# Shifted copies of score tiles moved from VectorE to GpSimd as 32-bit integer adds, in an order that treats the shared SBUF port as a lock

## The chip, the cores and the metric

The kernel runs on one core of one Trainium2 chip. Times are device microseconds. A median is over the runs of one kernel. A ratio is the mean time of one kernel's fast runs over that of the kernel before in the same rounds, with a 95% interval, so it is not quite the ratio of the medians that are quoted. The span of a profile is 1 to 3 us shorter than the time of its run.

A core has TensorE (PE), ScalarE (ACT), VectorE (DVE), GpSimd (POOL) and the DMA queues. They run side by side and wait for each other through semaphores; a port to the on-chip memory SBUF that VectorE and GpSimd share makes those two wait as well, and this case is about it. PSUM is the other on-chip memory; this kernel uses it in banks, and TensorE writes all its results there.

## The reference, cut to what matters

Two independent parts are computed and laid side by side in the output. The first is a state-space layer (2048 steps, 640 channels). The second is an attention layer with 32 heads that share one key and one value head:

```python
q = (x @ wq).reshape(B, S, 32, 20).transpose(0, 2, 1, 3)
k = x @ wk ; v = x @ wv
scores = einsum("bhqd,bkd->bhqk", q, k) * 20 ** -0.5
p = softmax(scores)
o = einsum("bhqk,bkd->bhqd", p, v) ; out = o.transpose(...).reshape(...) @ wo
```

With 32 heads, 16 blocks of 128 keys and 4 blocks of 512 queries there are 32 x 16 x 4 = 2048 score tiles of 128x512, and each element of them needs an exponential.

## The kernel before

A Python program (the planner) plays through the kernel with planned durations: at each step it gives a free engine the most urgent piece of work that is ready. It then writes out one fixed instruction order for each engine, with the semaphores that this order needs. The plan decides, tile by tile, who makes the exponentials:

* **ScalarE tiles.** TensorE writes scores into PSUM in chunks of three and two tiles. ScalarE takes the exponential of a chunk, from PSUM into SBUF. TensorE then multiplies it with the values.
* **VectorE tiles.** TensorE writes one score tile to a PSUM bank. VectorE adds a constant and stores it as a 16-bit integer, whose bits read as bf16 are a rough exponential ("eviction" below). Three more copies of the tile, with 32, 64 and 96 added, are made from SBUF to SBUF. TensorE multiplies all four with scaled values and sums them, which averages the error. Such a tile costs four value products in place of one.

```python
class Build:
    CHUNKS = (3, 2)     # PSUM banks of ScalarE's two score slots
    MISC = 2            # PSUM banks for VectorE tiles AND all background work
    NDS = 18            # SBUF buffers for evicted and copied tiles
    SHARE = 0.25        # at most this share of the tiles goes to VectorE
    SHIFTS = ((0, 0.2421875), (32, 0.201171875), (64, 0.169921875), (96, 0.142578125))
    # ... cut

    def want_d(self, taken=0):           # may the next tile be a VectorE tile?
        s = self.s
        if self.tile_n >= NTILE - 8 or self.d_count + taken + 1 > self.SHARE * (self.tile_n - 16):
            return False
        if len(self.d_banks()) <= taken:                           # a free PSUM bank
            return False
        return len(self.d_free()) > taken + len(self.SHIFTS) - 1    # free SBUF buffers

    def fill_d(self, op, m):
        # ... cut
        first = self.dve(self.ts(p.DR[:, h.index, :], bank.ap, 16256.0, 0.0, ALU.add, ALU.max), 605, deps=[op],
                         reads=[bank.key], writes=[key], prio=self.P1)
        self.s.spawn(self.d_give(bank, first))
        self.d_open.append([h, first, list(range(1, n)), b, kc, j])
        self.d_left[b, j] += n - 1
        self.pv_entry(b, kc, j, 0, h, first)

    def copy(self, op, k, tiles):        # one copy, or two tiles in one instruction
        # ... cut
        op.fns.append(self.ts(at(dst), at(src), float(self.SHIFTS[k][0]), 0.0, ALU.add, ALU.max))
```

The two `MISC` banks also serve the background work: query projections, the state-space products and the output projections. The number of VectorE tiles, D below, is thus fixed when the program is written out.

## Time and profile before

Median 787.37 us (786.44 to 789.14, 4 runs). In the profile (span 786.0 us):

| quantity | value | where it is read |
|---|---|---|
| ScalarE busy | 764.3 us, 97% | page, part 1 |
| ScalarE's exponentials | 1652 tiles, 747.4 us, 0.452 us each | groups |
| VectorE busy | 736.9 us, 94% | page, part 1 |
| VectorE tiles | 396 of 2048 (19.3%) | groups, evictions |
| GpSimd busy | 13.5 us, 2% | page, part 1 |

The page's busy line of the kernel before, then three of its groups. In a group, the columns are line, engine, operation, output and input, shapes and count; then busy time, mean ns of one; then idle time of the engine just before, and who ended it.

```profile
PE 727.8 (93%) x10253; PEld 237.8 (30%) x10253; DVE 736.9 (94%) x1765; ACT 764.3 (97%) x686; POOL 13.5 (2%) x35
...
L1015 ACT ACTIVATE PR<-SC 128x1024 bf16<-128x1024 f32 (+1 forms) x661 | 747.4, 1456 | 4.9 <-PE MB L546 2.6
...
L561 DVE TENSOR_SCALAR DR<-MB 128x512 int16<-128x512 f32 x396 | 262.7, 680 | 16.2 <-PE MB L546 14.1
L561 DVE TENSOR_SCALAR DR<-DR 128x512 int16<-128x512 int16 (+1 forms) x821 | 239.2, 342 | 2.9 <-PE MB L546 0.4
```

661 exponentials make 1652 tiles. The chain that ended last, by engine, and then the same engines in three steady stretches (busy us of each stretch; the count of instructions in brackets; PEclk is the granted share of TensorE's full clock):

```profile
ACT 90%; PE 5%; DVE 3%; DMA 1%; issue 0%; ACTq 0%; DVEq 0%
```

```profile
core 0: us, PE busy (x) PEld busy (x) DVE busy (x) ACT busy (x) POOL busy (x), PEclk, DMA share, GB/s
170.00:400.00 230.00, 217.41 (x3127) 70.29 (x3123) 221.86 (x507) 229.47 (x204) 0.00 (x0) 1.00 0.07 18
400.00:550.00 150.00, 142.86 (x2087) 46.34 (x2091) 143.84 (x343) 150.00 (x135) 0.00 (x0) 1.00 0.09 21
550.00:740.00 190.00, 176.83 (x2569) 57.26 (x2561) 178.02 (x426) 189.53 (x169) 0.00 (x0) 1.00 0.06 18
```

ScalarE is full in the steady stretches: 229.47 of 230, 150.00 of 150, 189.53 of 190. It is what bounds the kernel. So the span can be written as 786.0 - 747.4 = 38.6 us of start and tail, plus 0.4524 us for each of the 2048 - D tiles that are not among the D VectorE tiles. What this change can do is to raise D, unless it makes ScalarE wait.

VectorE's timeline from 100 us shows what a VectorE tile costs when instructions follow each other:

```profile
start us, us, engine line op out<-in xcount [idle before <-releaser]
...
100.02 1.27 DVE L561 TENSOR_SCALAR DR<-MB 128x512 int16<-128x512 f32 x2
101.22 0.41 DVE L561 TENSOR_SCALAR DR<-DR 128x1024 int16<-128x1024 int16 x1
...
103.76 1.08 DVE L561 TENSOR_SCALAR DR<-DR 128x1024 int16<-128x1024 int16 x3
104.76 0.68 DVE L561 TENSOR_SCALAR DR<-MB 128x512 int16<-128x512 f32 x1
```

Two evictions reach from 100.02 to 101.22, so 0.60 us each; three pair copies reach from 103.76 to 104.76, where the next instruction starts, so about 0.335 each.

The start of the trace has an instance that fits the shared port. The first line is GpSimd's timeline, the second VectorE's:

```profile
12.25 1.67 POOL L561 TENSOR_SCALAR fr<-iota,sc 128x512 int32<-128x512 f32 x2 [3.35 <-DVE sc L560]
```

```profile
12.66 0.71 DVE L560 TENSOR_SCALAR aq<-QT 128x512 int16<-128x512 int16 x1
```

The mask (`aq`) of 128x512 on VectorE takes 0.71 us while GpSimd works, where its group mean is 0.296 us.

### The profile page before, as it was taken

What the parts mean: (1) busy time and instruction counts of PE and PEld (TensorE: products, weight loads), DVE (VectorE), ACT (ScalarE), POOL (GpSimd) and SP (SyncE); (2) the same over time, 40 slices, a digit from 0 to 9 for tenths busy, and PEclk for the clock granted to TensorE, in tenths of its full rate; (3) what the DMA queues carried; (4) which work ended last, traced back from release to release, by engine and by line L of the source; (5) the groups of instructions that cost most, each with busy time, mean ns of one, the idle gap of its engine ahead of it and who ended that gap; (6) DMA issues with size and microseconds to landing.
All of it is one profiled execution on the core that took longest, in us unless ns stands there. A gap on an engine that the chain in (4) does not pass through costs nothing.

```text
span 786.0 us, 23805 instructions
## 1 busy us (share of the span) xinstructions
PE 727.8 (93%) x10253; PEld 237.8 (30%) x10253; DVE 736.9 (94%) x1765; ACT 764.3 (97%) x686; POOL 13.5 (2%) x35
## 2 busy tenths in 40 slices
PE   8988998889988999999999999999998999899887
PEld 3322222222223332323323222223222322233223
DVE  5999999999999999999998999999899999988995
ACT  5899999999999999999999999999999999999995
POOL 6000000000000000000000000000000000000000
PEclk9999999999999999999999999999999999999999
DMA  9840000020000000010000000010000000000001
GB/s 209 122 87 8 9 9 8 9 45 9 9 9 16 23 9 29 17 42 23 10 15 16 23 23 22 19 33 17 10 16 8 23 23 15 22 24 22 16 6 39
DMA packets 54184, 21.57 MB, mean 27 GB/s; under 512 B 43464, under 2 KB 54080, under 8 KB 54080
## 3 DMA queue, kind: packets, MB, share of 16 engines
q1 hardware_dynamic: 52072, 19.87, 11.4%
q8 instruction: 81, 1.33, 0.7%
q10 hardware_dynamic: 2008, 0.18, 0.2%
q14 instruction: 23, 0.19, 0.1%
HBM read 7.20 MB, written 5.50 MB: 16 GB/s over the span
## 4 chain that ended last, share of the span: by engine, by line
ACT 90%; PE 5%; DVE 3%; DMA 1%; issue 0%; ACTq 0%; DVEq 0%
ACT PR L1015 89%; PE SC L546 2%; PE MB L546 2%; DVE DR L561 1%; PE MB L542 1%; DMA vrow<-in_A_Dskip_dram 1%; PE SC L542 1%; DVE prod L556 0%; DVE WO L691 0%; DVE xbT L768 0%; DMA dn<-sums 0%; DMA sums<-pvsb 0%; ACTq L527 0%; DVE fr L561 0%; DVE g L1503 0%
## 5 line engine op out<-in xcount | busy, mean ns | idle before, releaser
L1015 ACT ACTIVATE PR<-SC 128x1024 bf16<-128x1024 f32 (+1 forms) x661 | 747.4, 1456 | 4.9 <-PE MB L546 2.6
L546 PE MATMUL SC<-QT,KT 32*128 32x512 bf16 x1652 | 257.8, 384 | 46.8 <-ACT PR L1015 33.0
L561 DVE TENSOR_SCALAR DR<-MB 128x512 int16<-128x512 f32 x396 | 262.7, 680 | 16.2 <-PE MB L546 14.1
L561 DVE TENSOR_SCALAR DR<-DR 128x512 int16<-128x512 int16 (+1 forms) x821 | 239.2, 342 | 2.9 <-PE MB L546 0.4
L546 PE MATMUL MB<-DR,VS 128*32 128x512 bf16 x1584 | 230.8, 384 | 0.2 <-DVE DR L561 0.2
L546 PE MATMUL MB<-PR,VP 128*32 128x512 bf16 x1652 | 226.6, 386 | 2.4 <-DVE pvsb L1207 1.8
L546 PEld LDWEIGHTS SC<-QT,KT 32*128 32x128 bf16 x1652 | 66.5, 91 | 298.6 <-ACT PR L1015 227.5
L546 PE MATMUL MB<-QT,KT 32*128 32x512 bf16 x396 | 143.8, 384 | 2.0 <-DVE DR L561 1.0
L546 PEld LDWEIGHTS MB<-PR,VP 128*32 128x32 bf16 x1652 | 56.8, 94 | 69.7 <-issue 50.3
L546 PEld LDWEIGHTS MB<-DR,VS 128*32 128x32 bf16 x1584 | 56.6, 94 | 55.6 <-issue 33.8
L542 PE MATMUL MB<-xaT,BT 128*32 128x512 bf16 x800 | 60.5, 382 | 0.2 <-DVE DR L561 0.2
L556 DVE TENSOR_TENSOR prod<-MB,Z 128x1024 bf16<-128x1024 f32 x40 | 48.6, 1216 | 2.7 <-PE MB L542 2.2
L546 PE MATMUL MB<-xbT,wqf 128*32 128x512 bf16 x640 | 47.9, 389 | 0.3 <-DVE DR L561 0.2
L542 PE MATMUL MB<-WO,OT 128*32 128x128 bf16 (+1 forms) x928 | 41.8, 292 | 0.0
L546 PEld LDWEIGHTS MB<-QT,KT 32*128 32x128 bf16 x396 | 34.2, 91 | 19.9 <-DVE DR L561 9.0
L1503 DVE TENSOR_TENSOR_SCAN g<-sc,hst,u 128x512 bf16<-128x512 f32 x30 | 38.0, 1273 | 0.0
L546 PE MATMUL MB<-KT,VZ 128*32 128x256 bf16 x656 | 33.8, 274 | 0.0
L542 PE MATMUL MB<-CT,xbT 128*32 128x512 bf16 (+1 forms) x640 | 31.9, 301 | 0.0
L542 PE MATMUL MB<-CT,W 128*32 128x512 bf16 (+1 forms) x640 | 31.5, 301 | 0.0
L556 DVE TENSOR_TENSOR prod<-g,tab 128x1024 bf16<-128x1024 bf16 x40 | 27.0, 680 | 0.0
L1207 DVE CAST pvsb<-MB 128x512 bf16<-128x512 f32 x32 | 21.9, 683 | 5.2 <-PE MB L546 5.2
L1326 DVE CAST stg<-MB 128x512 bf16<-128x512 f32 x35 | 23.9, 682 | 1.0 <-PE MB L542 0.8
(122 smaller groups left out, 340.9 us busy)
## 6 DMA issues: line engine op xcount, KB each, us to landing
out_dram<-stg SPq DMA_DIRECT2D x35, 128.0 KB, 1.7
rdB<-recs SPq DMA_DIRECT2D x124, 32.0 KB, 1.9
CT<-in_B_x_dram SPq DMA_DIRECT2D x2, 640.0 KB, 5.7
WO<-in_B_wo_dram SPq DMA_DIRECT2D x4, 200.0 KB
wqf<-in_B_wq_dram SPq DMA_DIRECT2D x1, 680.0 KB, 5.5
out_dram<-PR SPq DMA_DIRECT2D x5, 128.0 KB, 2.4
sums<-pvsb SPq DMA_DIRECT2D x31, 4.0 KB
dn<-sums SPq DMA_DIRECT2D x31, 4.0 KB, 1.8
```

What stands on the lines that cost most here:

```text
L542: r = e.matmul(out[32 * j:32 * j + 32], lhsT=lhsT[:, 32 * j:32 * j + 32], rhs=rhs, start=start, stop=stop, tile_position=(0, 32 * j), skip ...
L546: return lambda e: e.matmul(out, lhsT=lhsT, rhs=rhs, start=start, stop=stop, **kw)
L556: return lambda e: e.tensor_tensor(out, a, b, op)
L561: return lambda e: e.tensor_scalar(out, a, s1, s2, op0=op0, op1=op1)
L1015: ex = self.act(lambda e: e.activation(dst, t[:, 0:512 * n], ACT.Exp, scale=1.0 / UNIT), 0.8333 * 512 * n + 50, deps=[op], reads=[b.key fo ...
L1207: ev = self.dve(lambda e: e.tensor_copy(p.pvsb[:, slot, :], bank.ap), 620, deps=[op], reads=[bank.key], writes=[f"pvsb{slot}"], prio=self. ...
L1326: ev = self.dve(lambda e: e.tensor_copy(st, bank.ap), 620, deps=[prev], reads=[bank.key], writes=[key], prio=self.EV, gate=(lambda: last.e ...
L1503: o = self.dve(lambda e, ri=ri, init=init: e.tensor_tensor_scan(p.g[:, u, ri, :], rdec, p.u[:, ri, :], init, ALU.mult, ALU.add), 1280, dep ...
```

## The change

GpSimd, idle so far, shall make most of the copies. Two 16-bit values are added at once as one 32-bit integer add, since the sums never carry from the low half into the high one; two tiles go into one instruction. VectorE copies only when at least nine copies are waiting, or to close a block. GpSimd and those VectorE operations that use VectorE's second SBUF port exclude each other, so the plan gives every operation a mark `port` and never runs two marked ones on the two engines at once. Core of the diff (the mark `port=True` on a dozen more lines of VectorE operations is cut):

```diff
@@ Schedule.begin
+        if op.port:
+            if eng == "pool" and self.port_last["dve"] is not None:
+                op.after.append(self.port_last["dve"])
+            self.port_free[eng] = self.t + op.dur + (self.LOCK if eng == "pool" else 0.0)
+            self.port_last[eng] = op
+            # ... cut
@@ Schedule.pick
             if r <= t + 1e-6:
+                if op.port:
+                    if self.port_free["pool" if eng == "dve" else "dve"] > t + 1e-6:
+                        if eng == "dve":
+                            held.append(op)
+                        continue
+                    if eng == "pool" and self.port_wanted:
+                        continue
                 can.append(op)
+        # ... cut: port_wanted, true while VectorE holds back more urgent port work
@@ copy_source
+        if sum(len(d[2]) for d in can) < self.BACKLOG and not (can[0][3] == self.pv_b and self.pv_filled[self.pv_b] == 64):
+            return None
-        return Op("dve", [], 200 if one else 333, prio=prio, hook=lambda op: self.copy(op, k, two))
+        return Op("dve", [], 200 if one else 333, prio=prio, port=True, hook=lambda op: self.copy(op, k, two))
+    BACKLOG = 9
+    def pool_source(self):
+        # ... cut: two tiles that need the same shift, two free buffers, else None
+        return Op("pool", [], self.POOL2, prio=1, port=True, hook=lambda op: self.copy(op, k, two, True))
+    POOL2 = 1040.0
@@ copy
+            add = bass.AP(tensor=p.step, offset=k, ap=[[4, 128], [0, 2], [0, 256]])
+            op.fns.append(self.tt(words(dst), words(src), add, ALU.add))
@@ background
-                T.append((t, 1, lambda b=8 * qb + gg: self.tile_n >= 64 * (b - 11), ...
+                T.append((t, 1, lambda b=8 * qb + gg: self.tile_n >= 64 * (b - 11) and all((b // 8, c) in self.xb_op for c in range(NC)), ...
```

The Trainium skill, "GPSIMD Engine Reference", section "Engine selection", states that a GpSimd add with both inputs and the output of one 32-bit integer type is an exact integer add.

More of the change, by code (lines that the diff above doesn't have):

```diff
@@ L24 @@
     __slots__ = ("eng", "fns", "dur", "deps", "prio", "reads", "writes", "prev", "gate", "hook", "start", "end",
-                 "seq", "land", "dma_key", "idx", "tail", "mode", "load", "late")
+                 "seq", "land", "dma_key", "idx", "tail", "mode", "load", "late", "port", "after")
     def __init__(self, eng, fns, dur, deps=(), prio=5, reads=(), writes=(), prev=None, gate=None, hook=None,
-                 dma_key=None, land=0.0, tail=0.0, mode="F", load=0.0):
+                 dma_key=None, land=0.0, tail=0.0, mode="F", load=0.0, port=False):
         self.eng, self.fns, self.dur = eng, list(fns), dur
@@ L34, in __init__ @@
         self.mode, self.load, self.late = mode, load, False
+        self.port, self.after = port, []
         self.start = self.end = None
@@ L53 @@
     PAUSE = 3300.0
+    LOCK = 60.0
     def __init__(self):
@@ L68, in __init__ @@
         self.slack = {"pe": 60.0, "dve": 150.0}
+        self.port_free = {"dve": 0.0, "pool": 0.0}
+        self.port_last = {"dve": None, "pool": None}
+        self.port_wanted = False
     def recent(self, span):
@@ L126, in begin @@
             self.loads.append((self.t, op.load))
+        if op.port:
[3 more added lines that the diff above has]
+            self.port_last[eng] = op
+            self.at(self.port_free[eng])
         if op.dma_key is not None:
@@ L147, in pick @@
                 cands = cands + [extra]
-        can = []
+        can, held = [], []
         for op in cands:
@@ L171, in pick @@
                 best, key = op, (p, op.seq)
+        if eng == "dve":
+            self.port_wanted = any(best is None or op.prio < best.prio for op in held)
         return best
@@ L246, in dep @@
                     need[src] = o
+            for o in op.after:
+                dep(o)
             for k in op.writes:
@@ L468, in alloc @@
         self.lift = sb(o, "lift", [128, 4], FP32)
+        self.step = sb(o, "step", [128, 4], I32)
         self.mab = sb(o, "mab", [128, 8], FP32)
@@ L598, in program @@
         self.s.sources["dve"].append(self.copy_source)
+        self.s.sources["pool"].append(self.pool_source)
     def warm_source(self):
@@ L661, in constants @@
         many("VS", fns, 250)
+        many("step", [lambda e, k=k, c=c: e.memset(p.step[:, k:k + 1], c * 65537) for k, (c, _) in enumerate(self.SHIFTS)], 100)
         many("VZ", [lambda e: e.memset(p.VZ[:], 0.0)], 100)
@@ L891, in qt_task @@
         aq = self.dve(self.ts(p.aq[:, gg % 4, :].bitcast(I16), dst.bitcast(I16), 0x7FFF, None, ALU.bitwise_and), 200,
-                      deps=[ev], reads=[key],
+                      deps=[ev], reads=[key], port=True,
                       writes=[f"aq{gg % 4}"], prio=0.4 if first else 2, gate=lambda: self.aq_free(qb, gg))
@@ L1132, in copy_source, with copy @@
             prio = self.CLOSE
-        return Op("dve", [], 200 if one else 333, prio=prio, hook=lambda op: self.copy(op, k, two))
-    def copy(self, op, k, tiles):
+        return Op("dve", [], 200 if one else 333, prio=prio, port=True, hook=lambda op: self.copy(op, k, two))
+    BACKLOG = 9
+    def pool_source(self):
+        s = self.s
+        can = [d for d in self.d_open if d[1].end is not None and s.seen(d[1], "pool") <= s.t]
+        if not can or len(self.d_free()) < 2:
+            return None
+        k = can[0][2][0]
+        two = [d for d in can if k in d[2]][:2]
+        if len(two) < 2:
+            return None
+        return Op("pool", [], self.POOL2, prio=1, port=True, hook=lambda op: self.copy(op, k, two, True))
+    POOL2 = 1040.0
+    def copy(self, op, k, tiles, pool=False):
         p = self
@@ L1144, in at, with words @@
             return bass.AP(tensor=p.DR, offset=512 * x[0], ap=[[512 * p.NDS, 128], [512 * (x[1] - x[0]), 2], [1, 512]])
-        op.fns.append(self.ts(at(dst), at(src), float(self.SHIFTS[k][0]), 0.0, ALU.add, ALU.max))
+        if pool:
+            def words(x):
+                return bass.AP(tensor=p.DR, offset=512 * x[0], ap=[[512 * p.NDS, 128], [512 * (x[1] - x[0]), 2], [1, 512]]).bitcast(I32)
+            add = bass.AP(tensor=p.step, offset=k, ap=[[4, 128], [0, 2], [0, 256]])
+            op.fns.append(self.tt(words(dst), words(src), add, ALU.add))
+            op.reads.append("step")
+        else:
+            op.fns.append(self.ts(at(dst), at(src), float(self.SHIFTS[k][0]), 0.0, ALU.add, ALU.max))
         op.reads += [f"DR{i}" for i in src]
@@ L1237, in normalize @@
         ot = b % 10
-        self.norm_op[b] = self.dve(self.tt(p.OT[:, ot, :], p.pvsb[:, slot, :], p.rdB[:, slot, :], ALU.mult), 350, deps=[o],
+        self.norm_op[b] = self.dve(self.tt(p.OT[:, ot, :], p.pvsb[:, slot, :], p.rdB[:, slot, :], ALU.mult), 350, deps=[o], port=True,
                                    reads=[pv, rb], writes=[f"OT{ot}"], prio=self.EV, gate=lambda: self.ot_free(b))
@@ L1437, in ssm_scalars @@
             zs = []
-            o = self.dve(self.ts(t0, sin, gim, None, ALU.mult), 250, deps=[tabs[c], sc_op] + ([o] if c else []), reads=[tk, "sc"],
+            o = self.dve(self.ts(t0, sin, gim, None, ALU.mult), 250, port=True, deps=[tabs[c], sc_op] + ([o] if c else []), reads=[tk, "sc"],
                          writes=["prod3"], prio=3)
@@ L1441, in ssm_scalars @@
             o = self.dve(lambda e, c=c, cos=cos, gre=gre, t0=t0: e.scalar_tensor_tensor(
-                out=p.Z[:, 0, c, :], in0=cos, scalar=gre, in1=t0, op0=ALU.mult, op1=ALU.add), 650, deps=[o],
+                out=p.Z[:, 0, c, :], in0=cos, scalar=gre, in1=t0, op0=ALU.mult, op1=ALU.add), 650, deps=[o], port=True,
                 reads=[tk, "sc", "prod3"], writes=[zk], prio=3)
             zs.append(o)
-            o = self.dve(self.ts(t1, sin, gre, None, ALU.mult), 250, deps=[o], reads=[tk, "sc"], writes=["prod3"],
+            o = self.dve(self.ts(t1, sin, gre, None, ALU.mult), 250, port=True, deps=[o], reads=[tk, "sc"], writes=["prod3"],
                          prio=3)
@@ L1448, in ssm_scalars @@
             o = self.dve(lambda e, c=c, cos=cos, gim=gim, t1=t1: e.scalar_tensor_tensor(
-                out=p.Z[:, 1, c, :], in0=cos, scalar=gim, in1=t1, op0=ALU.mult, op1=ALU.subtract), 650, deps=[o],
+                out=p.Z[:, 1, c, :], in0=cos, scalar=gim, in1=t1, op0=ALU.mult, op1=ALU.subtract), 650, deps=[o], port=True,
                 reads=[tk, "sc", "prod3"], writes=[zk], prio=3)
@@ L1454, in ssm_scalars @@
             self.tab_op[c] = o
-        self.neg_op = self.dve(self.ts(p.CT[:, 1, :, :], p.CT[:, 1, :, :], -1.0, None, ALU.mult), 900,
+        self.neg_op = self.dve(self.ts(p.CT[:, 1, :, :], p.CT[:, 1, :, :], -1.0, None, ALU.mult), 900, port=True,
                                deps=[self.ct_op[1]], reads=["CT1"], writes=["CT1"], prio=3)
@@ L1495, in unit_rest @@
         for ri, op in ((0, ALU.subtract), (1, ALU.add)):
-            us.append(self.dve(self.tt(p.u[:, ri, :], p.prod[:, 0, ri, :], p.prod[:, 1, ri, :], op), 350, deps=prods,
+            us.append(self.dve(self.tt(p.u[:, ri, :], p.prod[:, 0, ri, :], p.prod[:, 1, ri, :], op), 350, deps=prods, port=True,
                                prio=3, reads=["prod0", "prod1"], writes=[f"u{ri}"], gate=self.gate_of("u")))
@@ L1503, in unit_rest @@
             o = self.dve(lambda e, ri=ri, init=init: e.tensor_tensor_scan(p.g[:, u, ri, :], rdec, p.u[:, ri, :], init,
-                                                                          ALU.mult, ALU.add), 1280,
+                                                                          ALU.mult, ALU.add), 1280, port=True,
                          deps=[us[ri]] + ([self.state_op[(tb - 1, c)]] if tb else []), prio=3.2 + 0.1 * ri,
@@ L1512, in unit_rest @@
             ck = f"ctmp{u}"
-            a = self.dve(self.ts(p.ctmp[:, u, :], p.rot[:, c, 0, :], p.g[:, u, 0, 511:512], None, ALU.mult), 130,
+            a = self.dve(self.ts(p.ctmp[:, u, :], p.rot[:, c, 0, :], p.g[:, u, 0, 511:512], None, ALU.mult), 130, port=True,
                          deps=[scans[0]], reads=[gk[0], "sc"], writes=[ck], prio=3.1)
@@ L1516, in unit_rest @@
                                                           scalar=p.g[:, u, 1, 511:512], in1=p.ctmp[:, u, :],
-                                                          op0=ALU.mult, op1=ALU.add), 130, deps=[a, scans[1]],
+                                                          op0=ALU.mult, op1=ALU.add), 130, deps=[a, scans[1]], port=True,
                          reads=[gk[1], "sc", ck], writes=[f"hst{c}"], prio=3.1)
@@ L1523, in unit_rest @@
             src = bass.AP(tensor=p.g, offset=1024 * u + 512 * ri, ap=[[2048, 128], [0, 2], [1, 512]])
-            o = self.dve(self.tt(p.prod[:, 2 + ri, :, :], src, self.pair(p.tab, c, ri), ALU.mult), 630,
+            o = self.dve(self.tt(p.prod[:, 2 + ri, :, :], src, self.pair(p.tab, c, ri), ALU.mult), 630, port=True,
                          deps=[scans[ri], self.tab_op[c]], prio=3, reads=[gk[ri], f"tab{c}"],
@@ L1529, in unit_rest @@
         for ri, op in ((0, ALU.subtract), (1, ALU.add)):
-            w = self.dve(self.tt(self.w_of(tb, c, ri), p.prod[:, 2, ri, :], p.prod[:, 3, ri, :], op), 350, deps=outs,
+            w = self.dve(self.tt(self.w_of(tb, c, ri), p.prod[:, 2, ri, :], p.prod[:, 3, ri, :], op), 350, deps=outs, port=True,
                          prio=3, reads=["prod2", "prod3"], writes=[f"W{c}_{tb % 2}"], gate=lambda: tb != 1 or self.first_half_read())
@@ L1597, in background @@
                 t = -100 + gg if qb == 0 else (qb - 1) * 512 + 40 + 50 * gg
-                T.append((t, 1, lambda b=8 * qb + gg: self.tile_n >= 64 * (b - 11), lambda bank, qb=qb, gg=gg: self.qt_task(qb, gg, bank)))
+                T.append((t, 1, lambda b=8 * qb + gg: self.tile_n >= 64 * (b - 11) and all((b // 8, c) in self.xb_op for c in range(NC)), lambda bank, qb=qb, gg=gg: self.qt_task(qb, gg, bank)))
                 if gg % 4 == 3:
```

## The prediction

> **What bounds the kernel now.** ScalarE. The chain of waits puts 89% of the 786.0 us span on its exponentials; the table by stretches has it busy 229.5 of 230 us (170 to 400) and 145.0 of 145 us (625 to 770). The groups give 747.4 us for 1652 score tiles: 0.452 us a tile. The other 38.6 us are start and tail. The remaining 396 of 2048 tiles go through VectorE: one eviction from PSUM and three shifted copies each. VectorE is the second bound: 736.9 us (94%). The share of 25% allowed (about 508 tiles) is not reached (19.3%) because VectorE has no time. Span, from these numbers: 38.6 + 0.452 x (2048 - D), D being VectorE tiles.
>
> **What one VectorE tile costs.** By start-to-start distances in the timeline: eviction 0.60 us, pair copy 0.335, single copy 0.23. 396 evictions 238 us, 367 pairs and 454 singles 227 us, all else about 272 us.
>
> **What the change moves.** I expect 65 to 80% of the copies on GpSimd, 370 to 500 pair adds. GpSimd is now idle (13.5 us). Its one-input 128x512 operations take 0.79 us here; the Trainium skill, "GPSIMD Engine Reference", section "Performance versus the Vector engine", gives about 2.6 cycles an element at 1.2 GHz for two inputs: 512 words, 1.1 us (estimate; this trace has no such operation). The order assumes 1.04. VectorE loses about 150 us of copies.
>
> **What it adds.** "SBUF — State Buffer", section "Who interferes with whom", says that GpSimd and those VectorE operations that use two SBUF ports or two SBUF inputs exclude each other for the whole instruction. The trace agrees at the start: a VectorE mask of 128x512 took 0.71 us beside a GpSimd operation, against 0.30 on average. So GpSimd fits only under VectorE's PSUM reads: 0.60 D + about 135 us (products, casts) = 415 us at D = 465. 400 adds of about 1.1 us are 440 us: an exact fit would need perfect packing. The lock is then held about 440 + 130 (scans, products, sums from SBUF) + 100 (copies left on VectorE) = 670 of some 725 us. I expect 60 to 100 us of VectorE time lost waiting for it. TensorE gets three more value products per extra tile, in groups of four: 0.75 x 0.22 us, 11 us for 70 tiles; its 34 us of filler can shrink.
>
> **Critical path.** The gain is only what leaves ScalarE: 0.452 us per tile. At the full share: 735 us. Waits at the lock, the 18 buffers held longer, and two PSUM banks keep it below: I expect D about 460 (440 to 490), so 38.6 + 0.452 x 1588 = 757 us, plus a little new ScalarE idleness from drift between planned and real GpSimd times: **760 us**, 8 in 10 within 742 to 781. Chances: faster by over 2% 0.70, within 2% 0.22, slower 0.08.
>
> **What would show it.** Groups: exponentials down to about 1590 tiles with ScalarE still near 100% in the steady stretches; evictions about 460; VectorE copies under 500 tiles; 370 to 500 GpSimd adds of 1.0 to 1.1 us. VectorE's copies, scans and sums longer in mean than now (pairs 0.415, scans 1.27, sums 0.41 us) where they meet GpSimd. Evictions unchanged at 0.68.
>
> **What would make it wrong.** A real add well over 1.1 us: every late copy delays products and buffers in an order fixed beforehand, VectorE stalls in order at the lock, PSUM banks come free late and ScalarE starves; the time could stay at 785 or rise. An add nearer 0.8 us, or good packing, would bring D to the cap and 737 us. TensorE, 93% busy, could become the limit near 500 tiles.

## The result, and the profile after

Median 781.07 us (780.03 to 782.19, 4 runs), 0.9922 of the kernel before, interval 0.9903 to 0.9941: 0.8% faster where 3.5% was predicted. The profile (span 778.8 us), busy line and groups as before:

```profile
PE 729.3 (94%) x10150; PEld 236.7 (30%) x10150; DVE 657.7 (84%) x1249; ACT 757.5 (97%) x680; POOL 380.0 (49%) x395
...
L1040 ACT ACTIVATE PR<-SC 128x1536 bf16<-128x1536 f32 (+1 forms) x655 | 740.7, 1427 | 2.8 <-PE MB L569 1.8
L579 POOL TENSOR_TENSOR DR<-DR,step 128x512 int32<-128x512 int32 x356 | 366.1, 1049 | 380.6 <-DVE DR L584 163.0
L584 DVE TENSOR_SCALAR DR<-MB 128x512 int16<-128x512 f32 x412 | 274.6, 685 | 75.5 <-PE MB L569 71.8
...
L584 DVE TENSOR_SCALAR DR<-DR 128x1024 int16<-128x1024 int16 (+1 forms) x289 | 105.3, 418 | 4.0 <-PE MB L569 3.1
```

```profile
ACT 80%; PE 13%; DVE 5%; DMA 1%; issue 1%; POOL 0%; ACTq 0%; DVEq 0%; POOLq 0%
```

```profile
170.00:400.00 230.00, 217.63 (x3111) 69.88 (x3107) 204.55 (x359) 229.28 (x205) 102.85 (x99) 1.00 0.07 18
400.00:550.00 150.00, 142.89 (x2068) 45.47 (x2060) 123.81 (x223) 149.85 (x134) 77.14 (x75) 1.00 0.08 21
550.00:740.00 190.00, 179.53 (x2575) 57.17 (x2571) 152.65 (x275) 189.77 (x169) 107.85 (x106) 1.00 0.06 19
```

* The adds work as costed: 356 of them, 1.049 us each. 712 of the 3 x 412 = 1236 copies (58%) are made by GpSimd.
* VectorE is relieved: 736.9 to 657.7 us busy, 94% to 84%. Taken apart: copies 239.2 to 105.3 (-133.9), evictions 262.7 to 274.6 (+11.9), the remainder 235.0 to 277.8 (+42.8), together -79.2. The remainder is not all new work: instructions that follow each other overlap in the profile (evictions of 0.68 us start 0.60 us apart), the total counts an overlap once, and with more gaps less is overlapped. By the means of the operations the rise is about 19 us (below).
* ScalarE is as full as before (229.28 of 230), and its idle time before exponentials even fell, from 4.9 to 2.8 us. So there is no new wait on the critical engine. TensorE's share of the chain rose from 5% to 13%, but if TensorE held ScalarE up more than before, this idle time would have grown.
* But VectorE tiles went only from 396 to 412. 16 x 0.4524 = 7.2 us is the whole gain: 786.0 - 7.2 = 778.8 us, the measured span; that it agrees to the last digit is chance, since the four runs span 778.0 to 780.1 us.

So the question is not where time was lost, but why VectorE's freed 79 us did not become more tiles. The waits of the changed kernel (engine, line, released by; total us, times, longest):

```profile
POOL DR L579 <- DVE DR L584: 163.0, 66, 27.0
DVE DR L584 <- PE MB L569: 75.0, 132, 2.6
POOL DR L579 <- DVE g L1553: 58.9, 19, 11.9
```

GpSimd stands 163.0 us waiting for VectorE's evictions and copies, and 58.9 us for scans. The group of evictions above has 75.5 us of VectorE idleness in front of it, 71.8 of it ended by TensorE; before it was 16.2 us. VectorE now waits for scores to evict, so its own time is no longer what is short. The direct price of the port on VectorE is visible in operations that meet an add. The sum of two SBUF tiles (`u`; duration ns min/median/max), before and after:

```profile
L556 DVE TENSOR_TENSOR u<-prod x40: 353/416/426, 101.6 to 665.4; 128x512 bf16<-128x512 bf16 x40
```

```profile
L579 DVE TENSOR_TENSOR u<-prod x40: 401/419/1284, 98.4 to 660.3; 128x512 bf16<-128x512 bf16 x40
```

Its maximum went from 426 to 1284 ns, its median hardly moved: collisions do happen, but the order dodges most of them. Over `u`, the normalisation, the mask, the products from SBUF, the small state updates, the scans and the sums `W`, the rise of the means times the counts is about 19 us, and 7 us on the 235 pair copies (446 against 415 ns).

### The profile page after: what moved, and what is told of

The parts are those of the page before. It is cut to its first block, busy times and chain, and to the rows that moved or that the text cites. A ratio compares the mean times of both kernels' runs of the same rounds, so it can differ in the third digit from the quotient of the medians.

```text
span 778.8 us, 23548 instructions
## 1 busy us (share of the span) xinstructions
PE 729.3 (94%) x10150; PEld 236.7 (30%) x10150; DVE 657.7 (84%) x1249; ACT 757.5 (97%) x680; POOL 380.0 (49%) x395
## 4 chain that ended last, share of the span: by engine, by line
ACT 80%; PE 13%; DVE 5%; DMA 1%; issue 1%; POOL 0%; ACTq 0%; DVEq 0%; POOLq 0%
ACT PR L1040 80%; PE MB L569 5%; PE SC L569 4%; PE MB L565 4%; DVE DR L584 1%; PE SC L565 1%; DMA vrow<-in_A_Dskip_dram 1%; DVE VS L583 0%; DVE xbT L793 0%; DVE WO L716 0%; DVE pvsb L1257 0%; DVE fr L584 0%; DVE QT L914 0%; DVE mab L814 0%; DVE sc L1404 0%
## 5 line engine op out<-in xcount | busy, mean ns | idle before, releaser
L1040 ACT ACTIVATE PR<-SC 128x1536 bf16<-128x1536 f32 (+1 forms) x655 | 740.7, 1427 | 2.8 <-PE MB L569 1.8
L579 POOL TENSOR_TENSOR DR<-DR,step 128x512 int32<-128x512 int32 x356 | 366.1, 1049 | 380.6 <-DVE DR L584 163.0
L584 DVE TENSOR_SCALAR DR<-MB 128x512 int16<-128x512 f32 x412 | 274.6, 685 | 75.5 <-PE MB L569 71.8
L569 PE MATMUL MB<-DR,VS 128*32 128x512 bf16 x1648 | 227.5, 385 | 2.6 <-DVE pvsb L1257 1.3
L569 PE MATMUL MB<-QT,KT 32*128 32x512 bf16 x412 | 151.2, 385 | 0.7 <-DVE DR L584 0.6
L584 DVE TENSOR_SCALAR DR<-DR 128x1024 int16<-128x1024 int16 (+1 forms) x289 | 105.3, 418 | 4.0 <-PE MB L569 3.1
L565 PE MATMUL MB<-CT,xbT 128*32 128x512 bf16 (+1 forms) x640 | 30.0, 301 | 0.0
L579 DVE TENSOR_TENSOR prod<-g,tab 128x1024 bf16<-128x1024 bf16 x40 | 29.4, 735 | 0.0
L569 PE MATMUL MB<-KT,VZ 128*32 128x256 bf16 x504 | 29.0, 279 | 0.0
```

The costliest lines, as they stand in the source:

```text
L565: r = e.matmul(out[32 * j:32 * j + 32], lhsT=lhsT[:, 32 * j:32 * j + 32], rhs=rhs, start=start, stop=stop, tile_position=(0, 32 * j), skip ...
L569: return lambda e: e.matmul(out, lhsT=lhsT, rhs=rhs, start=start, stop=stop, **kw)
L579: return lambda e: e.tensor_tensor(out, a, b, op)
L584: return lambda e: e.tensor_scalar(out, a, s1, s2, op0=op0, op1=op1)
L1040: ex = self.act(lambda e: e.activation(dst, t[:, 0:512 * n], ACT.Exp, scale=1.0 / UNIT), 0.8333 * 512 * n + 50, deps=[op], reads=[b.key fo ...
```

## The experiments

Eleven kernels ran beside the two. Theory A: the number of tiles is held down by the time for which adds hold the port, and above that by the two PSUM banks and TensorE, which VectorE tiles share with all other work. Theory B (rival): the order is too careful, or the chip drifts from the plan, and VectorE's time is still what counts.

The table collects all, with D counted in each profile (e7 and e8 have other chunks, to which the formula does not apply). "Formula" is 38.6 + 0.4524 x (2048 - D) (unrounded, 747.4 / 1652 for each tile), the span if ScalarE never waits longer than in the kernel before. Where the formula and the span agree, D alone explains the time.

| kernel | D | GpSimd adds | formula us | span us | median us | ratio to before, interval |
|---|---|---|---|---|---|---|
| before | 396 | 0 | 786.0 | 786.0 | 787.37 | |
| changed | 412 | 356 | 778.8 | 778.8 | 781.07 | 0.9922 (0.9903 to 0.9941) |
| e2, no GpSimd | 398 | 0 | 785.1 | 787.6 | 789.62 | 1.0017 (0.9991 to 1.0044) |
| e1, no lock in the plan | 449 | 523 | 762.0 | 878.3 | 880.33 | 1.1177 (1.1149 to 1.1204) |
| e4, half-width adds, one clearing | 448 | 575 | 762.5 | 776.7 | 778.52 | 0.9882 (0.9860 to 0.9903) |
| e5, half-width adds, 18 clearings | 449 | 542 | 762.0 | 777.3 | 781.60 | 0.9925 (0.9883 to 0.9968) |
| e9, half-width adds, no clearing | 446 | 525 | 763.3 | 768.2 | 769.99 | 0.9784 (0.9754 to 0.9815) |
| e3, no copies | 471 | 0 | 752.0 | 753.6 | 756.29 | 0.9597 (0.9574 to 0.9619) |
| e6, no copies, one product | 505 | 0 | 736.7 | 744.0 | 744.47 | 0.9452 (0.9407 to 0.9497) |
| e7, no copies, chunks (2, 2), two banks | 414 | 0 | | 807.5 | 809.67 | 1.0284 (1.0239 to 1.0329) |
| e8, no copies, chunks (2, 2), three banks | 478 | 0 | | 787.2 | 788.09 | 1.0020 (0.9961 to 1.0079) |
| e10, other constants | 427 | 358 | 772.0 | 774.4 | 776.05 | 0.9860 (0.9835 to 0.9886) |
| e11, backlog 99 | 415 | 402 | 777.4 | 793.0 | 793.43 | 1.0078 (1.0049 to 1.0107) |

D also answers to questions that need no chip. The planner of the two kernels, run again on a computer without a chip and with single constants changed, returns the D of every profile that was compared (396, 412, 449, 471, 505, 414, 478, 427), and besides:

* Buffers, a rival that no run tests, since copies that come late hold the 18 SBUF buffers longer: with 40 buffers in the plan (more than SBUF has room for) D is 395 in the kernel before, 413 in the changed one and 471 without copies. In these three plans buffers do not hold D down; in e1's, without the lock, 40 of them add ten tiles to 449.
* Scatter: with the add planned at 1000 to 1100 ns D goes from 402 to 420 without a trend. So differences of some eight tiles (396 and 398, 412 and 415) say nothing about a mechanism.
* Length of the add: planned at 800 ns, D is 428; at 620 ns, 444. Without the lock in the plan it is 449 at 1040 ns and 453 at 620 ns.

These are counts of plans, not times.

### e1: the same change without the lock in the plan

```diff
-        ... port=True ...
+        ... port=False ...        # everywhere
```

> The changed kernel with its lock model taken out of the order: no operation is marked as holding the shared port, so the list order lets GpSimd adds run beside any VectorE operation. The order then has 449 VectorE tiles and 523 adds (412 and 356 in the changed kernel). Theory A (the lock is real and most of the lost gain is paid to it): VectorE copies, scans and sums stretch wherever they meet an add (pair copy mean well over 0.6 us against 0.446 us), the eviction of a tile comes late, ScalarE waits for scores for tens of us, and the time is 775 us or more in spite of 37 more tiles. Theory B (the lock hardly costs; the order is too careful): 38.6 + 0.452 x (2048 - 449) = 761 us with ScalarE still full.

Measured: 880.33 us, correct result. The page's busy line and two groups:

```profile
PE 758.5 (86%) x10035; PEld 237.1 (27%) x10037; DVE 760.4 (87%) x1178; ACT 758.0 (86%) x665; POOL 609.1 (69%) x562
...
L1040 ACT ACTIVATE PR<-SC 128x1536 bf16<-128x1536 f32 (+1 forms) x640 | 741.1, 1266 | 101.4 <-PE MB L569 70.3
L579 POOL TENSOR_TENSOR DR<-DR,step 128x512 int32<-128x512 int32 x523 | 595.2, 1165 | 251.7 <-DVE DR L584 212.1
```

```profile
L579 DVE TENSOR_TENSOR u<-prod x40: 353/860/1265, 85.0 to 747.8; 128x512 bf16<-128x512 bf16 x40
```

ScalarE now idles 101.4 us before exponentials. The median sum `u` takes 860 ns against 416. The timelines at 100 us, GpSimd first, then three of the VectorE instructions inside that run of adds:

```profile
99.48 8.89 POOL L579 TENSOR_TENSOR DR<-DR,step 128x512 int32<-128x512 int32 x8
```

```profile
103.18 0.80 DVE L583 TENSOR_SCALAR ctmp<-rot,g 128x2 f32<-128x2 f32 x1
104.23 0.99 DVE L1565 SCALAR_TENSOR_TENSOR hst<-rot,g,ctmp 128x2 f32<-128x2 f32 x1
106.34 1.14 DVE L584 TENSOR_SCALAR DR<-DR 128x1024 int16<-128x1024 int16 x1
```

Two small state updates of two elements per partition take 0.80 and 0.99 us; in the kernel before their groups have means of 218 and 207 ns. Eight adds take 8.89 us, 1.11 each, so GpSimd is held up too. Theory A holds for the lock: it is real, and 37 more tiles are worth nothing when it is met blindly. "SBUF — State Buffer" of the Trainium skill, section "Who interferes with whom", says that the later one fully blocks; the trace agrees. It is also a first measure of what planning around the lock costs: the same planner, the same add of 1040 ns, without the lock 449 tiles, with it 412.

### e2: the rest of the change without GpSimd

```diff
-        self.s.sources["pool"].append(self.pool_source)
+        pass
-    BACKLOG = 9
+    BACKLOG = 0
```

and all `port=True` to `port=False`.

> The changed kernel with GpSimd's copies and the backlog rule off, the rest kept (the added condition on the query projections): 398 VectorE tiles. Both theories: within 0.5% of the kernel before, about 785 us, so that the whole gain of the change comes from the adds.

Measured: 789.62 us, ratio 1.0017: the same as before. The whole gain comes from the adds.

### e3: no copies at all

```diff
-        self.d_open.append([h, first, list(range(1, n)), b, kc, j])
-        self.d_left[b, j] += n - 1
-        self.pv_entry(b, kc, j, 0, h, first)
+        for k in range(n):
+            self.pv_entry(b, kc, j, k, h, first)
```

on the kernel before; the result is wrong (relative error 0.053).

> The kernel before with all shifted copies left out (the four products of a tile read the evicted tile itself; the result is wrong on purpose). This is the most that taking copies off VectorE can ever give. The order has 471 VectorE tiles, not the 508 of the allowed share. Theory A (something other than VectorE's time caps the number of tiles: the two PSUM banks that these tiles share with the other work, and TensorE's time for their products): ScalarE full, VectorE below 80%, 38.6 + 0.452 x 1577 = 752 us. Theory B (only VectorE's time limited it): it should come near 735 us.

Measured: 756.29 us.

```profile
PE 711.2 (94%) x9996; PEld 232.9 (31%) x9998; DVE 585.5 (78%) x1019; ACT 731.2 (97%) x656; POOL 13.5 (2%) x35
...
L1015 ACT ACTIVATE PR<-SC 128x1536 bf16<-128x1536 f32 (+1 forms) x631 | 714.4, 1434 | 5.6 <-PE MB L546 2.9
L561 DVE TENSOR_SCALAR DR<-MB 128x512 int16<-128x512 f32 x471 | 316.1, 686 | 108.2 <-PE MB L546 102.7
```

This is the ceiling for any way of moving copies with this planner and these constants (with slightly different look-ahead constants the plan has 462 to 475 tiles). With VectorE relieved of all of them, it is 78% busy and waits 108.2 us before evictions, nearly all for TensorE (102.7). Still the plan finds only 471 places for VectorE tiles. So VectorE's time is not all that holds D down, and that part of theory B fell; whether the order is too careful is left to e10.

### e4, e5, e9: adds of half the width

```diff
-    POOL2 = 1040.0
+    POOL2 = 540.0                                                 # 630.0 in e5, 620.0 in e9
-   ... ap=[[512 * p.NDS, 128], [512 * (x[1] - x[0]), 2], [1, 512]]).bitcast(I32)
-   add = bass.AP(tensor=p.step, offset=k, ap=[[4, 128], [0, 2], [0, 256]])
+   ... ap=[[512 * p.NDS, 128], [512 * (x[1] - x[0]), 2], [1, 256]]).bitcast(I32)
+   add = bass.AP(tensor=p.step, offset=k, ap=[[4, 128], [0, 2], [0, 128]])
```

The second half of a copied tile is then stale (wrong). So that nothing reads memory that was never written, e4 clears the buffers in one GpSimd instruction, e5 in 18, and e9 lets GpSimd write only buffers that VectorE has filled once.

> The changed kernel with adds of half the width (256 words, wrong result on purpose), planned with 540 ns in place of 1040; everything else, lock included, is kept. The order has 448 VectorE tiles and 575 adds. Theory A (the length of an add, for which it holds the port, costs the tiles): adds of about 0.54 us, 38.6 + 0.452 x 1600 = 762 us. Theory B (PSUM banks and TensorE alone set the 412 tiles, the port nothing): time as the changed kernel, about 781 us.

Measured: 778.52 us with 448 tiles. It missed: the exponentials began at 33.2 us, where those of the changed kernel begin at 24.4, because a VectorE instruction stood 7.86 us behind the clearing, which took 7.77.

> The half-width adds again (256 words, wrong result on purpose), now planned with their measured 0.63 us and with the long clearing of the buffers, which delayed the start of e4 by about 9 us, cut into short pieces. The order has 449 VectorE tiles and 542 adds, lock kept. Theory A (the time for which one add holds the port costs about 37 of the tiles): 38.6 + 0.452 x 1599 = 761 us, up to 770 with some idle ScalarE time; the exponentials start by 26 us. Theory B (the length of the add is not what counts): 778 to 782 us, as the changed kernel.

Measured: 781.6 us with 449 tiles; the exponentials began at 33.9 us. My cure was none. GpSimd's timeline, then VectorE's:

```profile
19.62 8.46 POOL L722 MEMSET DR<- 128x512 int16 x18
```

```profile
19.56 8.76 DVE L583 TENSOR_SCALAR trig<-sc 128x5 f32<-128x5 f32 x2 [0.51 <-POOL fr L584]
```

Two VectorE instructions on five elements per partition took 8.76 us beside 18 short clearings, one of them alone 8.55 (`--tile trig`). It did not get in between the clearings; why not was not tried.

> The half-width adds a third time (wrong result on purpose), now without clearing the buffers: GpSimd may only write buffers that VectorE has filled once. In e4 and e5 one VectorE operation stood for 8 us behind the clearing and the exponentials started at 33 us in place of 24. The order has 446 VectorE tiles and 525 adds. Theory A (the time for which one add holds the port costs about 35 tiles): exponentials start by 26 us and the time is 38.6 + 0.452 x 1602 = 763 us, up to 772. Theory B: 778 to 782 us, as the changed kernel.

Measured: 769.99 us, the exponentials from 24.4 us on.

```profile
L1040 ACT ACTIVATE PR<-SC 128x1536 bf16<-128x1536 f32 (+1 forms) x641 | 725.5, 1423 | 7.2 <-PE MB L569 6.7
L579 POOL TENSOR_TENSOR DR<-DR,step 128x256 int32<-128x256 int32 x525 | 310.6, 614 | 424.4 <-DVE DR L584 224.4
L584 DVE TENSOR_SCALAR DR<-MB 128x512 int16<-128x512 f32 x446 | 298.8, 685 | 85.7 <-PE MB L569 81.2
```

With adds of 0.614 us in place of 1.049 and the lock kept, the plan places 446 tiles in place of 412, and the time follows: 0.9784 of before against 0.9922. So the length of the add, at the lock, costs 34 tiles. A shorter add also delivers its copy earlier. That this is not the reason can be read from e1: there the plan had full-length adds without the lock, and placed 449; half-length ones without the lock bring it to no more than 453 (the counts above).

### e6: TensorE relieved

On top of e3:

```diff
-        for k in range(n):
-            self.pv_entry(b, kc, j, k, h, first)
+        h.left = 1
+        self.pv_entry(b, kc, j, 0, h, first)
```

> The kernel without copies (e3) with one value product per VectorE tile in place of four (wrong result on purpose): takes about 75 us of products off TensorE and changes nothing else; the two PSUM banks are as before. The order has 505 VectorE tiles, the allowed share. If TensorE's time for the three further products helps to cap the tiles at 471 when copies cost nothing: 38.6 + 0.452 x 1543 = 736 us. If only the PSUM banks cap them: 752 to 757 us as e3.

Measured: 744.47 us, over 8 us more than expected, with 505 tiles as expected; ScalarE idled 10.9 us before exponentials, and the mean granted clock of the profiled run was 0.972. With the same two banks, fewer products on TensorE lift D from 471 to the allowed share. A tile also gives its buffer back after one product in place of four, but buffers do not hold e3 down (471 with 40). So TensorE's time for the further products is part of the ceiling.

```profile
L1015 ACT ACTIVATE PR<-SC 128x1536 bf16<-128x1536 f32 x617 | 699.9, 1410 | 10.9 <-PE MB L546 7.5
L561 DVE TENSOR_SCALAR DR<-MB 128x512 int16<-128x512 f32 x505 | 337.6, 685 | 89.8 <-PE MB L546 82.0
```

### e7 and e8: one more PSUM bank

Both have no copies (wrong), on the changed kernel's code:

```diff
-    CHUNKS = (3, 2)
+    CHUNKS = (2, 2)
-    MISC = 2
+    MISC = 3                    # e8 only
```

> No copies (wrong result on purpose), with ScalarE's chunks of two and two tiles in place of three and two, one PSUM bank left unused: the control for e8. 414 VectorE tiles; ScalarE pays one overhead for two tiles, TensorE switches more often. About 800 us.

> As e7, with the unused bank given to the VectorE tiles and the background work (three in place of two). If the number of PSUM banks caps the VectorE tiles: 478 tiles in place of 414, and 15 to 20 us less than e7, about 783 us. If banks do not matter: as e7.

Measured on the same chip in the same rounds: 809.67 us with 414 tiles (e7) and 788.09 us with 478 (e8). The evictions of e7, then of e8:

```profile
L584 DVE TENSOR_SCALAR DR<-MB 128x512 int16<-128x512 f32 x414 | 281.0, 687 | 192.0 <-PE MB L569 190.0
L584 DVE TENSOR_SCALAR DR<-MB 128x512 int16<-128x512 f32 x478 | 323.1, 685 | 107.0 <-PE MB L569 102.5
```

One bank is worth 64 tiles and 21.6 us in this setting, and VectorE waits 85 us less for scores. So the banks hold D down too, shown with chunks of two and two. With chunks of three and two no run shows it: the eight banks that the kernel uses are all taken there. How the two parts divide is open.

### e11: still less work on VectorE

```diff
-    BACKLOG = 9
+    BACKLOG = 99
```

> The changed kernel with a backlog of 99 in place of 9: VectorE makes copies only for closing a block, so nearly all leave it. The order has 415 VectorE tiles and 402 adds. If VectorE's time were still what limits, it would be faster than the changed kernel. If the lock, the PSUM banks and TensorE limit: VectorE's busy share falls again (below 84%), the tiles stay near 412, copies come later, and the time is 785 to 792 us.

Measured: 793.43 us, slower than both kernels.

```profile
PE 735.4 (93%) x10117; PEld 237.4 (30%) x10119; DVE 650.1 (82%) x1210; ACT 757.4 (96%) x678; POOL 423.4 (53%) x441
...
L1040 ACT ACTIVATE PR<-SC 128x1536 bf16<-128x1536 f32 (+1 forms) x653 | 740.5, 1421 | 15.5 <-PE MB L569 14.2
L579 POOL TENSOR_TENSOR DR<-DR,step 128x512 int32<-128x512 int32 x402 | 409.5, 1041 | 349.7 <-DVE DR L584 140.0
L584 DVE TENSOR_SCALAR DR<-MB 128x512 int16<-128x512 f32 x415 | 277.8, 684 | 92.2 <-PE MB L569 88.1
```

GpSimd makes 402 pair copies in place of 356, VectorE's share falls to 82%, D is 415, and ScalarE waits 15.5 us before exponentials in place of 2.8. Taking work off VectorE beyond this point buys nothing. A likely reason, argued and not shown, is that a copy that waits for GpSimd's turn at the lock comes later than one that VectorE makes in 0.335 us.

### e10: the same change with other constants

```diff
-        self.slack = {"pe": 60.0, "dve": 150.0}
+        self.slack = {"pe": 100.0, "dve": 200.0}
-    LOCK = 60.0
+    LOCK = 30.0
-    SCARCE = 8
+    SCARCE = 5
-    BACKLOG = 9
+    BACKLOG = 7
-    POOL2 = 1040.0
+    POOL2 = 1020.0
```

The constants were picked by trying some hundreds of combinations for the shortest planned order, then one kernel with them was run. No such search was made for the kernel before, so 0.9860 is not the worth of the moved copies alone.

> The changed kernel with other constants of its order, chosen for the shortest planned order: backlog 7, add 1020 ns, pause at the lock 30 ns, look-ahead for urgent work 200 ns on VectorE and 100 ns on TensorE, five free buffers as the limit for scarce. Correct result. 427 VectorE tiles in place of 412: 0.452 x 15 = 6.8 us less than the changed kernel, 773 to 777 us, if a better fit of adds around the lock is what was missing; 781 us if the gain is lost to drift between plan and chip.

Measured: 776.05 us, correct result, 0.9860 of before: it beats both kernels.

```profile
L1040 ACT ACTIVATE PR<-SC 128x1536 bf16<-128x1536 f32 (+1 forms) x649 | 733.9, 1432 | 4.2 <-PE MB L569 2.8
L579 POOL TENSOR_TENSOR DR<-DR,step 128x512 int32<-128x512 int32 x358 | 368.9, 1050 | 372.4 <-DVE DR L584 172.0
L584 DVE TENSOR_SCALAR DR<-MB 128x512 int16<-128x512 f32 x427 | 283.1, 682 | 55.3 <-PE MB L569 49.6
```

The number of adds is nearly the same (358), but there are 15 more tiles than in the changed kernel, and VectorE is 87% busy. Which of the five constants did it was not tried, and the best of some hundreds of plans with such scatter is in part luck. Part of the lost tiles is thus the order's and not the chip's, as theory B had it. The span of 774.4 us is 2.4 above the formula, so the chip follows the plan here and drift is not what eats the gain.

## Why the prediction was wrong, point by point

* **ScalarE bounds, the gain is 0.452 us per moved tile: right.** 16 tiles, 7.2 us, and the span fell by 7.2 us.
* **Adds of 1.0 to 1.1 us: right** (1.049). **370 to 500 of them: a little high** (356). 65 to 80% of the copies: 58%.
* **"VectorE loses about 150 us of copies": about right** (133.9 us).
* **VectorE's port operations get longer, evictions do not: right** (evictions 685 against 680 ns). **"60 to 100 us of VectorE time lost waiting" at the lock: too high as a wait.** The means that I could compare add up to about 26 us. The plan avoids most collisions by holding operations back; the larger price is paid in tiles (e9), not in stretched instructions.
* **The share of 25% "is not reached (19.3%) because VectorE has no time", and from it "I expect D about 460 (440 to 490)": this step failed.** D is 412. A gain of 64 tiles was predicted, 16 came: 0.4524 x 48 = 21.7 us, which is the miss (760.0 against 781.07). I had converted VectorE's freed time into tiles and taken the lock and the banks as small deductions. What the runs showed in its place: VectorE stands 71.8 us waiting for scores before its evictions, and even with no copies at all, VectorE 78% busy, D is 471 (e3), so 460 needed the copies to cost nearly nothing. Half-length adds at the lock give 446, full-length ones 412. Of the mechanisms that I named, the lock and the banks were right and the 18 buffers were not; the deduction for them was 48 tiles from the cap of 508 where 96 were paid.
* **"TensorE, 93% busy, could become the limit near 500 tiles": wrong place.** TensorE's products already bind at 471 (e3, e6), and the banks bind in the setting of e7 and e8. I named 737 us, the cap of the allowed share, as the good end for "an add nearer 0.8 us, or good packing"; with no copies at all it is 756 us, and an add planned at 0.8 us brings the plan to 428 tiles.
* **"A little new ScalarE idleness from drift": did not come.** It fell from 4.9 to 2.8 us.

The exact share of each limit inside the 471 is open, and so is how much of the way from 412 to 471 a better order could still gain (e10: 15 tiles).

## What to carry to other kernels

When the work that is moved shares a port with the engine that it relieves, cost the port's time, not the relieved engine's: 356 adds at 1.05 us buy fewer tiles than VectorE's freed 79 us suggest. Before counting freed time as gain, ask what the next resource of the added work is, and measure the ceiling by leaving the moved work out altogether: e3 would have said at once that about 756 us was the best to hope for with this planner. Where a program fixes the decisive number before it runs, as it does D here, count it in the built program first: 412 could be had without a chip. An order that ignores such a lock can be far slower than no move at all (880 us), and where the order is planned, its constants deserve a new search after such a change (776 us, against a kernel before without such a search).

## What the Trainium skill lacked or had wrong

* "SBUF — State Buffer", "Who interferes with whom": it describes the port as held for the whole instruction. Here a VectorE instruction did not get in between 18 GpSimd clearings that followed each other: one VectorE instruction on 128x5 elements took 8.55 us beside 8.46 us of clearings (e5). In e1, between adds, VectorE's instructions did get in. What makes the difference was not tried (the adds read SBUF, the clearings only write it).
* "GPSIMD Engine Reference", "Performance versus the Vector engine": about 2.6 cycles an element for two inputs. The adds of 256 and 512 words with one broadcast operand have medians of 611 (e9) and 1037 ns (changed kernel): 426 ns for 256 words, 1.66 ns or 2.0 cycles at the page's 1.2 GHz, plus about 0.19 us fixed (an estimate from the two medians). The total of 1.05 us is close to the estimate of 1.1 all the same.
* No page says what to expect when VectorE's second-port work and GpSimd's together take most of the time: a planned exclusion cost 37 of 449 planned tiles here, an unplanned one 101.4 us of idle ScalarE (e1).
